# The last step of a layer norm on ScalarE, and its mean folded into the square

## The chip, the cores and the metric

One core of a Trainium2 chip runs the whole program. The metric is the device time of one execution in microseconds (us), lower is better. The engines are named as the profile names them: PE (TensorE matmul), PEld (TensorE weight load), DVE (VectorE), ACT (ScalarE), POOL (GpSimd) and SP (SyncE, which issues all DMAs here).

## What is computed

Three layers follow one another: an attention with a small state, a feed-forward layer with softmax-linear units and a layer norm (`_moe_ref`), and a feed-forward layer with squared relu (`_moe2_ref`). The change touches the middle one:

```python
def _moe_ref(x, w_in, w_out, g_ln):              # x: 4352 tokens of 512
    h = x @ w_in                                 # 1024 wide
    e = np.exp(h - h_max)
    solu = h * (e / (np.sum(e) + 1e-09))
    mu = np.mean(solu)
    var = np.mean((solu - mu) ** 2)
    ln = (solu - mu) / np.sqrt(var + 1e-06) * g_ln
    return ln @ w_out
```

All data is fp32; the big products split each operand into a rounded high part and a rest, and take three passes over them.

## The kernel before

**Tiling.** The tokens are taken in 8 batches of 512, four chunks of 128 tokens each, and two more chunks for the states at the end: 34 chunks in all. A chunk has its 128 tokens on the partitions and the 1024 hidden values of each along the free axis, in one tile `u`.

**Stages.** The first stage (the first 430 us of the profiled execution) computes attention and the middle layer. Its loop runs over the batches `b`; each iteration has eight steps `k`, one for each 128 of the 1024 hidden values. In a step, PE transposes the four chunks' finished `u` (`emit_lnT`, L684, into `lnTp`), ACT and DVE write the transposed tile as high part and rest into `lt` (L690 on ACT, then L693 on DVE), and PE multiplies the `lt` of the step before with `w_out` (`emit_l2`, L719, 12 matmuls into `y`). Between these come the first product of the next batch (`emit_l1`, L632, one chunk in each of four steps), the attention of the batch after that (`sT`, `ep`, `aT`, `srd`, `xs`, `sw`), and the decoding of the third layer's weights (`raw`, `dec`, `w2s`, with L312, L315, L318, and `copy` L262 and `sub` L268). The transposes of batch b+1 begin in step 7 of iteration b and need all four finished `u`. The second stage (430 us to the end) is the third layer, and uses nothing that the change touches.

**One chunk.** After its two halves are copied out of PSUM with a running minimum (`least`, L387, DVE), `solu_rest` does the rest: exp with the sum `es` on ACT (L592); the product of `u` and `e` with its sum `us` on DVE (L597); the negative mean `nmu` from `us`, a 128x1 operation on DVE (L600); the square of `u + nmu` with its sum `vs` on ACT (L603); four 128x1 operations on POOL (L611 to L618) that leave the reciprocal root in `c` (the tile `vs`); and last `u = (u + nmu) * c` (L621), on DVE or POOL, whichever is free earlier.

**What sets the order.** Each engine runs its instructions in the order in which the program emits them. PE's order is written out in the loops. For the others a planner (`Flow`) holds the open tasks; each request gives engines with a cost (`{"V": 0.75, "P": 1.7}`), and the planner emits it when its model says that operand and engine are free, the most urgent first. So a changed cost or engine of one request moves others too, and those DMAs on SP that depend on them.

Of the kernel before, what the change touches and what calls it, by code (L numbers as in the profile page):

```python
# [11 lines left out]
AF = mybir.ActivationFunctionType  # L12
ALU = mybir.AluOpType
# [151 lines left out]
def attn_solu_relu2_kernel(  # L165
# [14 lines left out]
    nc = tc.nc  # L180
# [6 lines left out]
    B, P, T, _ = x_n.shape  # L187
# [5 lines left out]
    DM, F1 = w_in.shape  # L193
# [388 lines left out]
    def solu_rest(u, nmx, last):  # L582
        def small(name):
            return smp.tile([P, 1], F32, tag=name, name=name, bufs=4)

        yield None, 0.0, lambda: last["done"] is not None
        f = last["done"]
        yield take("e")
        e_ = ep.tile([P, F1], F32, tag="e", name="e")
        es, us, nmu, vs = (small(n) for n in ("es", "us", "nmu", "vs"))  # L590
        q, c = es, vs
        f = yield {"A": 1.16}, f, lambda e: nc.scalar.activation(  # L592
            out=e_, in_=u, func=AF.Exp, bias=nmx, scale=-1.0, accum_out=es
        )

        def prod(e):
            nc.vector.scalar_tensor_tensor(  # L597
                out=u, in0=u, scalar=-1.0, in1=e_, op0=ALU.mult, op1=ALU.mult, accum_out=us
            )
            nc.vector.tensor_scalar(out=nmu, in0=us, scalar1=-1.0 / F1, scalar2=None, op0=ALU.mult)  # L600

        f = yield {"V": 1.33}, f, prod
        f = yield {"A": 1.16}, f, lambda e: nc.scalar.activation(  # L603
            out=e_, in_=u, func=AF.Square, bias=nmu, accum_out=vs
        )
        give("e")

        def root(e):  # L610
            nc.gpsimd.tensor_scalar(  # L611
                out=q, in0=es, scalar1=1e-9, scalar2=1e-3, op0=ALU.add, op1=ALU.mult
            )
            nc.gpsimd.tensor_tensor(out=q, in0=q, in1=q, op=ALU.mult)
            nc.gpsimd.tensor_scalar(
                out=c, in0=vs, scalar1=1.0 / F1, scalar2=q, op0=ALU.mult, op1=ALU.add
            )
            nc.gpsimd.tensor_tensor(out=c, in0=c, in1=mhalf, op=ALU.pow)  # L618

        f = yield {"P": 2.4}, f, root  # L620
        f = yield {"V": 0.75, "P": 1.7}, f, lambda e: eng_of[e].tensor_scalar(  # L621
            out=u, in0=u, scalar1=nmu, scalar2=c, op0=ALU.add, op1=ALU.mult
        )
        return f

# [752 lines left out]
```

## Time and profile before

| | before |
|---|---|
| median of three timed runs | 1113.36 us (1108.63 to 1115.36) |
| profiled execution | 1106.97 us, span 1105.2 us |
| mean granted clock of TensorE | 0.988 |
| busy: PE / DVE / ACT / POOL | 1067.7 / 803.5 / 557.0 / 163.3 us |
| busy of 385 us from 45 to 430: PE / DVE / ACT / POOL | 367.5 / 303.8 / 242.7 / 149.2 us |
| busy of 655.2 us from 450 to the end: PE / DVE / ACT / POOL | 650.4 / 450.1 / 276.9 / 0 us |

A busy time adds up the spans of an engine's instructions without overlap. PEclk is the clock that TensorE was granted, as a part of full speed (2.4 GHz); 0.50 is the lower of its two levels (1.2 GHz). A waiting instruction holds up all that stands behind it on its engine.

### The profile page before, as it was taken

To read this page: it belongs to the slowest core of one execution; us is meant where nothing else is said; L and a number is where in the kernel's file an instruction comes from. 1 tells how busy PE (TensorE), PEld (TensorE's weight loads), DVE (VectorE), ACT (ScalarE), POOL (GpSimd) and SP (SyncE) were. 2 spreads that over 40 slices of the span, in tenths; PEclk is the share of its full clock that TensorE was granted. 3 is DMA by queue.
4 is the path that set the end of the run, shared out by engine and by line. 5 is a ranking of instruction groups with operands and counts; after the bars stand their busy time and mean duration, and the time that the engine had idled before them with its cause. 6 is when DMAs were issued, how large, how long until landed. Compare 5 with 4: busy or idle time off the path is not lost.

```text
span 1105.2 us, 19405 instructions
## 1 busy us (share of the span) xinstructions
PE 1067.7 (97%) x7184; PEld 940.0 (85%) x7184; DVE 803.5 (73%) x1293; ACT 557.0 (50%) x960; POOL 163.3 (15%) x211
## 2 busy tenths in 40 slices
PE   4889999999999899999999999999999999999998
PEld 1467777767777688889998889999999999999998
DVE  6967789787797767877974578755688467855773
ACT  4846576676676546445453334543345334533442
POOL 1623245354453520000000000000000000000000
PEclk8989999999999899999999999999999999999999
DMA  9421464735625457998687767778888888898884
GB/s 350 166 84 44 155 240 148 276 123 208 236 91 218 173 180 241 303 329 278 188 254 226 194 195 213 229 221 273 252 274 289 291 254 274 273 305 253 252 257 153
DMA packets 126509, 247.70 MB, mean 224 GB/s; under 512 B 13520, under 2 KB 36048, under 8 KB 124368
## 3 DMA queue, kind: packets, MB, share of 16 engines
q1 hardware_dynamic: 126416, 246.47, 68.6%
q8 instruction: 57, 0.93, 0.4%
q14 instruction: 36, 0.29, 0.1%
HBM read 199.23 MB, written 47.19 MB: 223 GB/s over the span
## 4 chain that ended last, share of the span: by engine, by line
PE 78%; DVE 8%; DMA 6%; issue 3%; ACT 2%; POOL 2%; SPq 0%; ACTq 0%; POOLq 0%; DVEq 0%
PE h L1286 31%; PE h L1141 30%; PE y L719 10%; PE hps L632 4%; DMA w_d<-w2s 2%; DMA raw<-w_in 2%; DVE u L597 2%; PE lnTp L684 1%; DMA raw<-w_out 1%; DVE u L387 1%; PE hps L376 1%; DMA raw_u<-w_in 1%; POOL w2s L268 1%; DVE dec L318 1%; DVE lt L693 1%
## 5 line engine op out<-in xcount | busy, mean ns | idle before, releaser
L1286 PE MATMUL h<-w,g 128*128 128x256 f32 x2856 | 343.5, 283 | 0.0
L1286 PEld LDWEIGHTS h<-w,g 128*128 128x128 f32 x2856 | 343.3, 192 | 0.2
L1141 PE MATMUL h<-yt,w 128*128 128x384 f32 (+1 forms) x1680 | 328.2, 356 | 0.5 <-ACT ys L262 0.5
L1141 PEld LDWEIGHTS h<-yt,w 128*128 128x128 f32 x1680 | 300.5, 188 | 27.0 <-ACT ys L262 0.7
L719 PE MATMUL y<-lt,wo 128*128 128x512 f32 (+1 forms) x864 | 220.9, 397 | 3.6 <-DVE lt L693 3.3
L262 ACT CAST g<-r 128x768 fp32r<-128x768 f32 (+1 forms) x140 | 128.3, 920 | 149.5 <-PE h L1286 148.0
L719 PEld LDWEIGHTS y<-lt,wo 128*128 128x128 f32 x864 | 150.8, 192 | 40.8 <-issue 6.7
L268 DVE TENSOR_TENSOR g<-r,g 128x768 fp32r<-128x768 f32 (+1 forms) x140 | 148.4, 1063 | 51.0 <-ACT g L262 50.4
L1105 DVE TENSOR_TENSOR r<-u,h 128x384 f32<-128x384 f32 (+1 forms) x120 | 72.1, 604 | 110.2 <-PE h L1141 109.8
L1091 ACT COPY u<-h 128x512 f32<-128x512 f32 (+2 forms) x160 | 81.8, 524 | 112.8 <-PE h L1141 86.6
L1187 DVE TENSOR_TENSOR r<-r 128x768 f32<-128x768 f32 (+1 forms) x100 | 104.9, 1060 | 20.5 <-ACT r L1177 20.2
L632 PE MATMUL hps<-sw,aT 128*128 128x512 f32 x368 | 98.1, 415 | 0.6 <-DVE s_sb L387 0.6
L632 PEld LDWEIGHTS hps<-sw,aT 128*128 128x128 f32 x368 | 69.0, 190 | 24.4 <-issue 5.8
L693 DVE SCALAR_TENSOR_TENSOR lt<-lnTp,g_sb,lt 128x512 fp32r<-128x512 f32 (+1 forms) x72 | 51.4, 714 | 27.0 <-ACT lt L690 26.7
L690 ACT ACTIVATE lt<-lnTp,g_sb 128x512 fp32r<-128x512 f32 (+1 forms) x72 | 47.7, 663 | 42.3 <-PE lnTp L684 42.2
L1179 DVE SCALAR_TENSOR_TENSOR r<-r 128x768 f32<-128x768 f32 (+3 forms) x80 | 65.2, 835 | 1.2
L1091 ACT ACTIVATE r<-h 128x384 f32<-128x384 f32 (+1 forms) x40 | 21.3, 532 | 83.1 <-PE h L1141 82.7
L603 ACT ACTIVATE e<-u,nmu 128x1024 f32<-128x1024 f32 x34 | 39.1, 1149 | 20.9 <-DVE nmu L600 20.9
L684 PE MATMUL lnTp<-ident,u 128*128 128x128 f32 x272 | 42.8, 277 | 4.9 <-DVE u L621 2.8
L597 DVE SCALAR_TENSOR_TENSOR u<-u,e 128x1024 f32<-128x1024 f32 x34 | 44.0, 1295 | 4.0 <-ACT e L592 4.0
L268 DVE TENSOR_TENSOR yt<-yraw,yt 128x384 fp32r<-128x384 f32 (+1 forms) x70 | 41.3, 606 | 6.3 <-ACT yt L262 6.2
L268 POOL TENSOR_TENSOR w2s<-dec,w2s 128x512 fp32r<-128x512 f32 (+1 forms) x30 | 35.9, 1197 | 60.9 <-ACT w2s L262 59.7
(97 smaller groups left out, 922.4 us busy)
## 6 DMA issues: line engine op xcount, KB each, us to landing
w<-w_d SPq DMA_DIRECT2D x560, 256.0 KB, 3.3
w_d<-w2s SPq DMA_DIRECT2D x36, 512.0 KB, 3.8
raw<-w_out SPq DMA_DIRECT2D x24, 512.0 KB, 6.8
xT<-x_t SPq DMA_DIRECT2D x8, 1024.0 KB, 6.9
xn<-x_n SPq DMA_DIRECT2D x8, 1024.0 KB, 5.9
y_d<-ys SPq DMA_DIRECT2D x16, 512.0 KB, 3.2
raw<-w_in SPq DMA_DIRECT2D x16, 512.0 KB, 6.8
out<-u SPq DMA_DIRECT2D x28, 256.0 KB, 2.8
```

Source lines behind the costliest of these rows:

```text
L262: nc.scalar.copy(out=out, in_=in_)
L268: return lambda e: eng_of[e].tensor_tensor(out=out, in0=in0, in1=in1, op=ALU.subtract)
L597: nc.vector.scalar_tensor_tensor(out=u, in0=u, scalar=-1.0, in1=e_, op0=ALU.mult, op1=ALU.mult, accum_out=us)
L632: nc.tensor.matmul(out=ps, lhsT=lhsT(i, k), rhs=rhs(j, k)[:, cs], start=(k == 0 and n == 0), stop=(k == n_k - 1 and n == len(passes) - 1),)
L693: f = yield {"V": 0.1 + nt * 0.155}, f, lambda e: nc.vector.scalar_tensor_tensor(out=o[:, 1], in0=pf, scalar=gk, in1=o[:, 0].bitcast(F32), ...
L719: nc.tensor.matmul(out=ps, lhsT=wo[k][:, w, c * P:(c + 1) * P], rhs=o[:, a], start=(k == 0 and i == 0), stop=(k == K1 - 1 and i == 2),)
L1091: nc.scalar.activation(out=o, in_=src, func=func) if func else nc.scalar.copy(out=o, in_=src)
L1105: f = yield {"V": 0.15 + cols / 960}, max(at, box["task"]["done"]), lambda e: nc.vector.tensor_tensor(out=o, in0=box["t"], in1=src, op=ALU.add
L1141: nc.tensor.matmul(out=ps, lhsT=wt[:, e2, k], rhs=yy[:, e1, k], start=(p in ("P1", "P2", "P5") and k == 0 and s == 0), stop=(k == 1 and s ...
L1179: f = yield {"V": 0.15 + (2 - key[-1]) * q / 960}, f, lambda e: nc.vector.scalar_tensor_tensor(out=v, in0=v, scalar=0.0, in1=v, op0=ALU.ma ...
L1187: return lambda e: eng_of[e].tensor_tensor(out=out, in0=in0, in1=in1, op=op)
L1286: nc.tensor.matmul(out=where[i // 2][0][:, i % 2 * Q:i % 2 * Q + Q], lhsT=g[:, e1, m % 2, i * P:i * P + P], rhs=wt[:, e2], start=(p in ("P ...
```

## The change

The mean is no operation of its own any more. The square takes the sum `us` as its bias and `-n` as its scale (n = 1024), so that it sums (us - n u)^2, and the factor n^-3 in the third small POOL operation takes that back to the variance. POOL gets a fifth small operation, `nmu = -us / n * c`, and the last step becomes one ACT activation, `u = c * u + nmu`. The planner's costs change with it: 1.3 for the product, 2.7 for the root, and 1.16 on ACT alone for the last step.

```diff
         def prod(e):
             nc.vector.scalar_tensor_tensor(
                 out=u, in0=u, scalar=-1.0, in1=e_, op0=ALU.mult, op1=ALU.mult, accum_out=us
             )
-            nc.vector.tensor_scalar(out=nmu, in0=us, scalar1=-1.0 / F1, scalar2=None, op0=ALU.mult)
-
-        f = yield {"V": 1.33}, f, prod
+
+        f = yield {"V": 1.3}, f, prod
         f = yield {"A": 1.16}, f, lambda e: nc.scalar.activation(
-            out=e_, in_=u, func=AF.Square, bias=nmu, accum_out=vs
+            out=e_, in_=u, func=AF.Square, bias=us, scale=-n, accum_out=vs
         )
...
             nc.gpsimd.tensor_scalar(
-                out=c, in0=vs, scalar1=1.0 / F1, scalar2=q, op0=ALU.mult, op1=ALU.add
+                out=c, in0=vs, scalar1=n ** -3, scalar2=q, op0=ALU.mult, op1=ALU.add
             )
             nc.gpsimd.tensor_tensor(out=c, in0=c, in1=mhalf, op=ALU.pow)
-
-        f = yield {"P": 2.4}, f, root
-        f = yield {"V": 0.75, "P": 1.7}, f, lambda e: eng_of[e].tensor_scalar(
-            out=u, in0=u, scalar1=nmu, scalar2=c, op0=ALU.add, op1=ALU.mult
+            nc.gpsimd.tensor_scalar(
+                out=nmu, in0=us, scalar1=-1.0 / n, scalar2=c, op0=ALU.mult, op1=ALU.mult
+            )
+
+        f = yield {"P": 2.7}, f, root
+        f = yield {"A": 1.16}, f, lambda e: nc.scalar.activation(
+            out=u, in_=u, func=AF.Identity, bias=nmu, scale=c
         )
```

Counted over the whole program, DVE loses the 34 means, 10 of the last steps and 8 subtractions `w2s`, and gets two copies from ACT; POOL loses 24 of the last steps and gets 34 small operations and the 8 subtractions; ACT gets 34 activations and gives up the two copies. PE's order is the same, instruction for instruction. In the new kernel the lines from L592 on carry other numbers: exp L593, product L598, Square L603, the last step L624, `lt` L693 on ACT and L696 on DVE.

At the start, ACT's rows from the second chunk's square to the transposed tile of batch 0. Before, where the last step is on no ACT row:

```order
L603 ACTIVATE e,vs<-u,nmu 128x1024
L262 CAST wo_136<-dec 128x512
L592 ACTIVATE e,es<-u,hm 128x1024
L504 ACTIVATE sr<-srd,l_190 128x64 x2
L400 ACTIVATE eT,l_472<-s_sb,m_491 128x512
L262 COPY xs<-xsp 128x4x32
L262 CAST sw<-hps 128x512
L400 ACTIVATE eT,l_472<-s_sb,m_492 128x512
L262 COPY s_sb<-ep 128x512
L603 ACTIVATE e,vs<-u,nmu 128x1024
L262 COPY s_sb<-ep 128x512
L433 ACTIVATE a_sb<-a_sb 128x512
```

And now, at the same place:

```order
L593 ACTIVATE e,es<-u,hm 128x1024
L504 ACTIVATE sr<-srd,l_190 128x64 x2
L603 ACTIVATE e,vs<-u,us 128x1024
L400 ACTIVATE eT,l_477<-s_sb,m_490 128x512
L262 COPY xs<-xsp 128x4x32
L603 ACTIVATE e,vs<-u,us 128x1024
L262 COPY s_sb<-ep 128x512
L624 ACTIVATE u<-u,nmu,vs 128x1024
L400 ACTIVATE eT,l_477<-s_sb,m_491 128x512
L624 ACTIVATE u<-u,nmu,vs 128x1024 x2
L262 CAST sw<-hps 128x512
L693 ACTIVATE lt<-lnTp,g_sb 128x512
```

The last chunk's square stands two attention rows (`L400`, `s_sb`) earlier, three last steps stand behind it, and the softmax rows of the next batch's attention (`L433 a_sb`) come behind the first `lt` instead of ahead of it.

In iteration 3, ACT's rows around two successive `lt`. Before:

```order
L312 ACTIVATE dec<-raw 128x512
L433 ACTIVATE a_sb<-a_sb 128x512
L312 ACTIVATE dec<-raw 128x512
L603 ACTIVATE e,vs<-u,nmu 128x1024
L690 ACTIVATE lt<-lnTp,g_sb 128x512
L592 ACTIVATE e,es<-u,hm 128x1024
L262 COPY s_sb<-ep 128x512
L400 ACTIVATE eT,l_2232<-s_sb,m_2246 128x512
L433 ACTIVATE a_sb<-a_sb 128x512
L603 ACTIVATE e,vs<-u,nmu 128x1024
L690 ACTIVATE lt<-lnTp,g_sb 128x512
```

And now:

```order
L312 ACTIVATE dec<-raw 128x512
L433 ACTIVATE a_sb<-a_sb 128x512
L603 ACTIVATE e,vs<-u,us 128x1024
L693 ACTIVATE lt<-lnTp,g_sb 128x512
L312 ACTIVATE dec<-raw 128x512
L593 ACTIVATE e,es<-u,hm 128x1024
L262 COPY s_sb<-ep 128x512
L400 ACTIVATE eT,l_2224<-s_sb,m_2239 128x512
L624 ACTIVATE u<-u,nmu,vs 128x1024
L433 ACTIVATE a_sb<-a_sb 128x512
L603 ACTIVATE e,vs<-u,us 128x1024
L693 ACTIVATE lt<-lnTp,g_sb 128x512
```

The second decode (`L312`, which waits for a `raw` DMA) moves behind the first `lt`, and between the two `lt` there are now seven activations instead of five.

At the end of iteration 6, DVE's rows from the last chunk's second half (`hps,hm`) to the `lt` of step 7. `wil` are subtractions that only the last two chunks need later. Before:

```order
L387 TENSOR_SCALAR u,hm<-hps,hm 128x512
L693 SCALAR_TENSOR_TENSOR lt<-lnTp,g_sb,lt 128x512
L268 TENSOR_TENSOR wil<-wi_126,wih 128x512
L268 TENSOR_TENSOR wil<-wi_127,wih 128x512
L597 SCALAR_TENSOR_TENSOR u,us<-u,e 128x1024
L600 TENSOR_SCALAR nmu<-us 128x1
L693 SCALAR_TENSOR_TENSOR lt<-lnTp,g_sb,lt 128x512
```

And now:

```order
L387 TENSOR_SCALAR u,hm<-hps,hm 128x512
L696 SCALAR_TENSOR_TENSOR lt<-lnTp,g_sb,lt 128x512
L268 TENSOR_TENSOR wil<-wi_128,wih 128x512
L268 TENSOR_TENSOR wil<-wi_129,wih 128x512
L598 SCALAR_TENSOR_TENSOR u,us<-u,e 128x1024
L696 SCALAR_TENSOR_TENSOR lt<-lnTp,g_sb,lt 128x512
L268 TENSOR_TENSOR wil<-wi_126,wih 128x512
L696 SCALAR_TENSOR_TENSOR lt<-lnTp,g_sb,lt 128x512
```

The last chunk's half and product stand one `lt` and two `wil` earlier than they did, and one `wil` takes the product's place ahead of step 7's `lt`.

## Rows read from the trace of the kernel before

**Rows 1.** Busy time by stretch: length, PE, PEld, DVE, ACT, POOL, clock, DMA share, GB/s.

```profile
45.00:430.00 385.00, 367.52 (x2526) 284.60 (x2514) 303.84 (x612) 242.69 (x454) 149.20 (x192) 0.98 0.48 171
450.00:1105.20 655.20, 650.37 (x4451) 627.13 (x4449) 450.07 (x592) 276.94 (x442) 0.00 (x0) 1.00 0.81 251
```

**Rows 2.** Waits of PE, whole span: us in total, times, the longest.

```profile
PE sTp L414 <- DVE lt L693: 5.1, 3, 2.3
PE y L719 <- DVE lt L693: 3.3, 4, 1.9
PE lnTp L684 <- DVE u L621: 2.8, 1, 2.8
...
PE lnTp L684 <- POOL u L621: 1.7, 1, 1.7
```

**Rows 3.** Groups by line: busy us, mean ns of one, idle before.

```profile
L603 ACT ACTIVATE e<-u,nmu 128x1024 f32<-128x1024 f32 x34 | 39.1, 1149 | 20.9 <-DVE nmu L600 20.9
L621 POOL TENSOR_SCALAR u<-u,nmu,vs 128x1024 f32<-128x1024 f32 x24 | 34.7, 1444 | 2.5
L621 DVE TENSOR_SCALAR u<-u,nmu,vs 128x1024 f32<-128x1024 f32 x10 | 8.4, 841 | 1.5 <-POOL vs L618 1.5
L600 DVE TENSOR_SCALAR nmu<-us 128x1 f32<-128x1 f32 x34 | 5.2, 154 | 1.2
L615 POOL TENSOR_SCALAR vs<-vs,es 128x1 f32<-128x1 f32 x34 | 11.7, 345 | 68.7 <-ACT e L603 68.4
L268 POOL TENSOR_TENSOR w2s<-dec,w2s 128x512 fp32r<-128x512 f32 (+1 forms) x30 | 35.9, 1197 | 60.9 <-ACT w2s L262 59.7 <-DMA w_d<-w2s 1.2
```

**Rows 4.** The start, in order of time, PE and DVE: start, us, [idle before].

```profile
58.16 0.95 PE L684 MATMUL lnTp<-ident,u 128*128 128x128 f32 x5 [2.78 <-DVE u L621]
61.22 2.07 PE L719 MATMUL y<-lt,wo 128*128 128x512 f32 x4 [0.73 <-DVE lt L693]
...
57.39 0.72 DVE L621 TENSOR_SCALAR u<-u,nmu,vs 128x1024 f32<-128x1024 f32 x1
```

**Rows 5.** Iteration 3, in order of time: ACT and PE.

```profile
218.09 0.68 ACT L312 ACTIVATE dec<-raw 128x512 f32<-128x512 f32 x1 [1.41 <-DMA raw<-w_in]
220.22 0.68 ACT L312 ACTIVATE dec<-raw 128x512 f32<-128x512 f32 x1 [0.93 <-DMA raw<-w_in]
221.92 0.68 ACT L690 ACTIVATE lt<-lnTp,g_sb 128x512 fp32r<-128x512 f32 x1
228.12 0.67 ACT L690 ACTIVATE lt<-lnTp,g_sb 128x512 fp32r<-128x512 f32 x1
...
223.44 0.66 PE L414 MATMUL sTp<-ident,s_sb 128*128 128x128 f32 x4 [2.34 <-DVE lt L693]
```

**Rows 6.** Busy time between the two `lt` of ACT in iteration 3, columns as above.

```profile
221.92:228.12 6.20, 4.68 (x25) 3.99 (x26) 5.26 (x11) 4.78 (x12) 2.93 (x5) 1.00 0.00 0
```

**Rows 7.** The turn from iteration 6 to 7, in order of time: PE, DVE, POOL.

```profile
366.95 3.44 PE L719 MATMUL y<-lt,wo 128*128 128x512 f32 x14
372.29 1.79 PE L719 MATMUL y<-lt,wo 128*128 128x512 f32 x4 [1.90 <-DVE lt L693]
376.41 0.47 PE L684 MATMUL lnTp<-ident,u 128*128 128x128 f32 x1 [1.69 <-POOL u L621]
376.54 2.91 PE L719 MATMUL y<-lt,wo 128*128 128x512 f32 x6
...
366.99 2.16 DVE L268 TENSOR_TENSOR wil<-wi,wih 128x512 fp32r<-128x512 f32 x2
369.07 2.31 DVE L597 SCALAR_TENSOR_TENSOR u<-u,e 128x1024 f32<-128x1024 f32 x1
...
374.63 1.72 POOL L621 TENSOR_SCALAR u<-u,nmu,vs 128x1024 f32<-128x1024 f32 x1
```

**Rows 8.** Busy time and granted clock in two stretches, columns as above.

```profile
60.00:65.00 5.00, 4.27 (x13) 3.10 (x12) 3.18 (x7) 0.59 (x1) 1.30 (x2) 0.50 0.00 0
375.00:380.00 5.00, 3.59 (x12) 2.89 (x13) 4.31 (x6) 3.04 (x6) 4.36 (x3) 0.55 0.57 224
```

More of the change, by code (lines that the diff above doesn't have):

```diff
@@ L591, in solu_rest @@
         q, c = es, vs
+        n = float(F1)
         f = yield {"A": 1.16}, f, lambda e: nc.scalar.activation(
```

## The prediction

> **What bounds the kernel now.** I read the table of stretches first. PE is busy for 650.4 of the 655.2 us after 450, and PE's order is the same in both kernels, so nothing is to be gained or lost there [rows 1]. From 45 to 430 PE is busy for 367.5 of 385.0 us: 17.5 us of idle time are what better placed work could give back, and every new wait of PE in that stretch is a loss. DVE works 303.8 us there (79%), ACT 242.7 (63%), POOL 149.2 (39%). So PE is the bound all along, and the other engines count only where PE waits for them.
>
> The list of PE's waits says where that is [rows 2]: 5.1 us in three waits of `sTp` for DVE's `lt`, 3.3 in four waits of `y` for it, and 2.8 and 1.7 in two waits for a finished `u`. These make 12.9 of the 17.5 us. The rest waits for attention tiles.
>
> **What is removed, added and moved.** First the chain of one chunk, with no queue in it. The mean on DVE goes, 0.154 us ahead of the square. POOL's fifth small operation comes in; the trace does not hold it, and its nearest row is L615, the same form with a scalar operand from a tile, at 0.345 us; the bounds are 0.154 (the mean as DVE ran it) and twice the row, 0.69. The last step becomes an activation; the nearest row is the square, with the same shape and one operand from a tile fewer, at 1.149 us, in place of 1.444 on POOL (24 times) and 0.841 on DVE (10 times) [rows 3]. With these the chain changes by -0.154 + 0.345 + 1.149 - 1.444 = -0.10 us for 24 chunks, and by -0.154 + 0.345 + 1.149 - 0.841 = +0.50 for 10. In the mean that is +0.07 us per chunk: as a chain the change gives nothing. What it can give comes from the queues.
>
> The queues: DVE loses 34 x 0.154 + 10 x 0.841 = 13.6 us, and the 8 subtractions that go to POOL besides. POOL loses 34.7, and gets 34 x 0.345 + 8 x 1.197 = 21.3. ACT gets 34 x 1.149 = 39.1 us, and goes from 63% of the stretch to (242.7 + 39.1) / 385 = 73%, DVE from 79% to 75% or less. No engine passes PE over the whole stretch; the local steps decide.
>
> The Trainium skill prices this activation a little higher (ScalarE: Activation LUTs, What ACT_TABLE_LOAD costs): 186 ns + 0.833 ns an element, and 93 ns for each operand from a tile, an estimate of 1.23 us for 1024 elements and two operands. The square's row with one such operand agrees with it (1.13 by the page, 1.149 by the row), and 34 x 0.08 would put 2.7 us more on ACT, or 0.3 in an iteration.
>
> *The start.* PE's transposes for batch 0 wait 2.78 us until 58.16 for the last chunk's `u`, which DVE finishes at 57.39 + 0.72 = 58.11; then `y` waits until 61.22 for the rest part of `lt`, which lies behind other work on DVE [rows 4]. In the new order the last chunk's square stands ahead of two attention rows, and three last steps follow on ACT. Going down ACT's rows with the durations above, I get the last `u` at about 56.5, 1.6 earlier, and `lt`'s rest right behind it on DVE, some 2.8 earlier. The softmax rows (`L433`) now come behind the first `lt`, so the attention transposes that PE needs next are late instead; I take 2.0 of the 2.8. Bounds: 0 (the softmax takes it all) and 2.78 + 0.73 = 3.5 (both waits go).
>
> *The loop.* The largest of the three `sTp` waits is 2.34 us at 223.44 [rows 5]. DVE's `lt` is late because ACT's is (221.92), and that stands behind a square and, ahead of it, two decodes that wait for DMAs (1.41 and 0.93 us). The new order puts one last step ahead of the first decode, where it fits into the 1.41 us for which ACT waits for the DMA anyway, and the second decode, with 0.93 + 0.68 us, behind the `lt`. So this `lt` comes about 1.5 us earlier. Such a saving can't exceed its own wait, and the other two waits are some 1.4 each; I take 1.5 + 1.0 + 1.0 = 3.5 of 5.1 us (bounds 0 and 5.1). Where the cover fails, that is where the DMA has landed before ACT comes to the decode, the step costs its 1.149 us in full and the saving is 0.5.
>
> *The turn from iteration 6 to 7.* `y` waits 1.90 us for `lt` at 372.29, and a transpose 1.69 for the last `u` at 376.41 [rows 7]. Both stand behind one product on DVE, at 369.07 for 2.31 us. In the new order that product stands an `lt` and two subtractions (2.16 us in the trace) earlier, and `lt` is behind one subtraction and no longer behind the product. From the product to the finished `u` it takes 1.15 + 0.19 for the square and its sum, some 1.3 for POOL and 1.15 for the last step, 3.8 us. With the product ending at 368.4 or a little earlier, `u` is there at about 372.1, when PE comes to the transposes. Of 3.6 us I take 3.2 (bounds 0 and 3.6).
>
> *The clock.* In two short stretches TensorE is granted the lower level of its clock: 0.50 of full speed from 60 to 65 and 0.55 from 375 to 380 [rows 8], in both behind PE's idle time. Six matmuls took 2.91 us there and four 1.79, where 14 at full speed took 3.44: 6 x (0.485 - 0.246) + 4 x (0.448 - 0.246) = 2.2 us. If the turn's idle time goes, most of this goes too; I take 2.0 (bounds 0 and 2.2). At the start idle time stays, so I take nothing (bounds 0 and about 4, twice that sum, by the 5 us at 0.50).
>
> *New waits.* ACT is fuller, and each `lt` on it can be late behind a last step. Between the two `lt` at 221.92 and 228.12 ACT was busy for 4.78 of 6.20 us [rows 6]; the new order has one last step and one decode more there, 4.78 + 1.15 + 0.68 = 6.6, or about 6.3 where they overlap their neighbours by 0.1 each. This is the tightest place, and it comes once per iteration. PE has 12 matmuls of 0.246, 2.95 us [rows 7], between the transposes and the use of an `lt`, and `lt` takes 0.68 on ACT and as much on DVE: some 1.5 us of delay are hidden, and a slip of 0.1 to 0.4 is paid for in few steps. I put 2.0 us over all (bounds 0 and 0.4 x 7 = 2.8 without the rival below). The 8 subtractions that move to POOL delay SP's stores of `w2s` and the `raw` loads behind them on its queue; POOL is idle for 60% of the stretch, and a decode now stands later on ACT, so I price that at nothing; without that cover a `raw` load comes 1.197 us later.
>
> **Sum.** 2.0 + 3.5 + 3.2 + 2.0 - 2.0 = 8.7 us. The profiled execution took 1107.0 us, and would take 1098.3; the timed runs have a median of 1113.4, 6.4 above it. I take the saving from the median: 1113.4 - 8.7 = 1104.7 us.
>
> **Rivals.**
> - *Nothing comes of it* (0.25). The chain of one chunk is not shorter, and the `lt` waits are set by `raw` DMAs that no order of ACT speeds up. For it: the +0.07 us, and the waits in [rows 5]. Against: the turn's waits come from DVE's queue [rows 7], where no DMA is. Time: 1113, within 4.
> - *All waits go, and both clock stretches* (0.20). 3.5 + 5.1 + 3.6 + 2.2 + 4 = 18.4 us: 1095, between 1092 and 1100. For it: all of them stand behind `u` or `lt`. Against: some idle time at the start stays in my walk, and the clock fell there.
> - *ACT becomes the bound of the loop, and the kernel is slower* (0.10). The place is the pair of steps with a first product, a decode and attention rows on ACT. If the stall for `raw` (1.41 + 0.93) is not covered any more and adds to the 6.6 us of work in 6.2, ACT ends 2.7 us late, 1.2 beyond what PE can hide, and again in the step behind it: 2.4 x 7 = 17 us, 1130. It decides from about 1.5 us of delay on. For it: ACT's share of the tightest step. Against: the step ahead of it got a decode less. The Trainium skill would expect this one (ScalarE: Activation LUTs, Rules for kernel authors): it says that adds and multiplications belong on VectorE and not on ScalarE. The rows agree as to the single instruction, 0.841 against 1.149, but only 10 of 34 ran on DVE.
>
> **How the numbers follow.** The forecast, 5 to 13 us saved, has 0.45. The range from 1093 to 1116 leaves out the fastest third of the second rival (0.07), the third one (0.10) and a little of the first: about 0.2. One per cent is 11 us, about what a measurement of this kernel can tell from no change. Faster by more, under 1102.2, takes the second rival and a third of the forecast: 0.36. Slower by more takes most of the third rival: 0.09. The rest, 0.55, is within 1%.
>
> **What would show it.** In the new profile the last step should take 1.15 to 1.25 us on ACT, and POOL's fifth operation 0.2 to 0.7. PE's waits for `sTp` should fall from 5.1 us to under 2, those at the turn from 3.6 to under 1, with no clock under 0.9 near 375. The span of the second stage should stay at 655 within 1. I am wrong if PE's idle time from 45 to 430 is still 17 us, or if it waits for ACT's `lt` in most iterations.

## The result and the profile after

The changed kernel takes 1096.07 us (median of 6 runs, 1094.58 to 1096.98) against 1113.59 us for the kernel before in the same set (6 runs, 1108.63 to 1115.36): a ratio of 0.9855, with a 95% interval from 0.9831 to 0.9879. The profiled execution took 1096.98 us, with a span of 1095.1; that of before took 1106.97, with a span of 1105.2. So the two medians are 17.5 us apart, and the two profiled executions 10.0. Both numbers matter below. One execution of the kernel before, in the set of e10, took 1435.67 us at a mean clock of 0.687 and is left out of every comparison.

The line numbers after the change are up to three higher: the last step is L624, POOL's fifth operation L619, and `lt` is made on L693 and L696. The first view after is the table of stretches: length, busy time of each engine, granted clock, DMA share and GB/s. It answers to [rows 1] and [rows 8].

```profile
core 0: us, PE busy (x) PEld busy (x) DVE busy (x) ACT busy (x) POOL busy (x), PEclk, DMA share, GB/s
45.00:430.00 385.00, 375.53 (x2563) 293.13 (x2552) 294.43 (x573) 279.91 (x494) 129.21 (x208) 0.99 0.50 177
370.00:380.00 10.00, 10.00 (x50) 8.28 (x49) 7.61 (x13) 4.38 (x9) 5.12 (x5) 1.00 0.68 267
60.00:65.00 5.00, 5.00 (x17) 4.02 (x17) 2.67 (x5) 1.36 (x3) 3.52 (x3) 0.50 0.02 3
178.00:181.00 3.00, 3.00 (x10) 2.42 (x9) 2.56 (x4) 2.71 (x5) 0.40 (x2) 0.50 0.00 0
```

PE now sits idle for 9.5 of the 385 us, where it was 17.5. ACT has gone from 242.7 to 279.9 us and is at 73%; PE is not waiting for it more than before. The low clock near 375 is gone. The one behind 60 is still there, and there is a new one from 178 to 181 us, where the kernel before is granted 1.00.

The second view is the list of PE's waits over the whole span (in total, times, the longest), which answers to [rows 2].

```profile
...
PE sTp L414 <- DVE lt L696: 3.3, 1, 3.3
PE y L722 <- DVE sw L268: 1.7, 2, 1.1
...
PE lnTp L687 <- ACT u L624: 1.1, 2, 0.8
PE xsp L519 <- ACT sr L504: 1.0, 1, 1.0
...
PE y L722 <- DVE lt L696: 0.3, 1, 0.3
...
```

The 12.9 us of waits for `lt` and `u` have become 3.3 + 1.1 + 0.3 = 4.7, with 1.7 us of a new wait for `sw`, a part of the attention, at the start. What is left in the loop is one single wait of 3.3 us.

The third view is the groups by line, for the operations whose price the prediction had to take from neighbours [rows 3].

```profile
L624 ACT ACTIVATE u<-u,nmu,vs 128x1024 f32<-128x1024 f32 x34 | 42.1, 1241 | 2.5 <-POOL nmu L619 2.5
L603 ACT ACTIVATE e<-u,us 128x1024 f32<-128x1024 f32 x34 | 39.0, 1148 | 5.7 <-DVE u L598 5.5
L619 POOL TENSOR_SCALAR nmu<-us,vs 128x1 f32<-128x1 f32 x34 | 15.1, 445 | 3.5
```

The last step takes 1.241 us and the fifth small operation 0.445, where I had taken 1.149 and 0.345. The square waits 5.7 us in all for what comes ahead of it, where it waited 20.9: the mean no longer stands between the product and the square.

The fourth view is PE's longer waits in order of time, from 45 us to the end of the first stage: start, duration, tile and, in brackets, the wait.

```profile
47.92 0.33 PE L519 MATMUL xsp<-ident,sr 128*128 128x128 f32 x1 [1.00 <-ACT sr L504]
...
55.62 0.76 PE L687 MATMUL lnTp<-ident,u 128*128 128x128 f32 x5 [0.80 <-ACT u L624]
...
59.15 1.65 PE L722 MATMUL y<-lt,wo 128*128 128x512 f32 x3 [1.13 <-DVE sw L268]
177.59 0.93 PE L414 MATMUL sTp<-ident,s_sb 128*128 128x128 f32 x4 [3.29 <-DVE lt L696]
...
421.06 11.17 PE L1144 MATMUL h<-yt,w 128*128 128x512 f32 x48 [0.54 <-ACT ys L262]
```

Between 178 and 407 us PE doesn't wait at all. The turn from iteration 6 to 7, with its 1.90 and 1.69 us [rows 7], passes without a gap. The second stage begins at 421.06 instead of 430.19 us, and from there to the end it takes 674.0 us instead of 675.0. The difference of 1.0 us lies behind PE's last matmul, which ends 4.8 us ahead of the end of the span before and 3.9 now; up to there the second stage is as it was.

### The profile page after: what moved, and what is told of

Read it like the earlier page. It is cut to its first block, busy times and chain, and to the rows that moved or that the text cites. A ratio compares the mean times of both kernels' runs of the same rounds, so it can differ in the third digit from the quotient of the medians.

```text
span 1095.1 us, 19407 instructions
## 1 busy us (share of the span) xinstructions
PE 1065.5 (97%) x7184; PEld 941.0 (86%) x7184; DVE 786.7 (72%) x1243; ACT 589.4 (54%) x992; POOL 144.2 (13%) x229
## 4 chain that ended last, share of the span: by engine, by line
PE 89%; ACT 4%; DVE 3%; DMA 2%; issue 1%; POOL 1%; SPq 0%; ACTq 0%; DVEq 0%; POOLq 0%
PE h L1289 31%; PE h L1144 30%; PE y L722 15%; PE hps L635 7%; PE lnTp L687 2%; PE hps L376 1%; DMA raw_u<-w_in 1%; ACT u L624 1%; PE aTp L470 1%; DMA raw<-w_in 1%; ACT e L603 1%; PE srd L486 1%; PE sTp L414 0%; DMA raw<-w_out 0%; PE sps L376 0%
## 5 line engine op out<-in xcount | busy, mean ns | idle before, releaser
L696 DVE SCALAR_TENSOR_TENSOR lt<-lnTp,g_sb,lt 128x512 fp32r<-128x512 f32 (+1 forms) x72 | 51.6, 716 | 25.6 <-ACT lt L693 24.8
L1182 DVE SCALAR_TENSOR_TENSOR r<-r 128x768 f32<-128x768 f32 (+3 forms) x80 | 65.2, 834 | 1.2
L693 ACT ACTIVATE lt<-lnTp,g_sb 128x512 fp32r<-128x512 f32 (+1 forms) x72 | 47.7, 662 | 31.4 <-PE lnTp L687 31.3
L268 POOL TENSOR_TENSOR w2s<-dec,w2s 128x512 fp32r<-128x512 f32 (+1 forms) x38 | 47.9, 1273 | 70.3 <-ACT w2s L262 50.3
L598 DVE SCALAR_TENSOR_TENSOR u<-u,e 128x1024 f32<-128x1024 f32 x34 | 42.5, 1249 | 5.9 <-ACT e L593 5.5
L624 ACT ACTIVATE u<-u,nmu,vs 128x1024 f32<-128x1024 f32 x34 | 42.1, 1241 | 2.5 <-POOL nmu L619 2.5
```

The lines of the kernel that those rows point to most:

```text
L268: return lambda e: eng_of[e].tensor_tensor(out=out, in0=in0, in1=in1, op=ALU.subtract)
L624: f = yield {"A": 1.16}, f, lambda e: nc.scalar.activation(out=u, in_=u, func=AF.Identity, bias=nmu, scale=c)
L1182: f = yield {"V": 0.15 + (2 - key[-1]) * q / 960}, f, lambda e: nc.vector.scalar_tensor_tensor(out=v, in0=v, scalar=0.0, in1=v, op0=ALU.ma ...
```

## The experiments

My theory after the result was that of the prediction, sharpened. The loop waits where ACT, which runs its work strictly in order, has a decode (L312) ahead of an `lt`, and the decode's `raw` DMA has not landed. The change moves decodes behind the `lt`, and the turn is freed of one late product. The rivals: it is the load taken from VectorE or from POOL, or it is the fold of the mean.

### The kernel before against itself

The unchanged kernel, to see what a difference of this size is worth and how far its executions differ.

> The kernel before, unchanged, so that its executions are seen with their clock. Theory 1 (its executions differ: idle time of PE before a transpose or an attention tile sometimes brings a further stretch at the lower clock): times of 1107 to 1116 us, and the longer ones at a lower mean clock, 0.988 for 1107 and 0.980 or less for 1114. Theory 2 (the profiled execution of this kernel was just a lucky one in its DMA waits): the same spread at an unchanged clock of 0.988. Theory 3 (a profiled execution is always some 6 us faster than a timed one): the profile is again at 1107 and every timed run at 1113.

Measured: 1110.77 us (12 runs, 1107.49 to 1115.54), ratio 1.0 (0.9983 to 1.0017). The executions of before differ by 8 us among themselves, and the three longest (1112.81, 1114.16 and 1115.54) have the lowest mean clock, 0.984, against 0.985 to 0.989 for the others: the first theory holds in part. The third is refuted, since the profiled execution is above the median here. It took 1112.53 us, 5.6 more than the profiled one that the prediction was read from, and its list of PE's waits has this row:

```profile
PE sTp L414 <- DVE lt L693: 7.5, 4, 2.4
```

That is four waits and 7.5 us, against three and 5.1 in [rows 2]. In iterations 3 to 6 (180 to 360 us) ACT stood 16.8 us ahead of its 16 decodes in this execution, and 13.6 in the other. So 2.4 of the 5.6 us are the very waits that the change is about: the execution I predicted from was one with few of them. Of the rest, 1.5 us are a low stretch of the clock behind one of these waits (0.51 from 223.2 to 226.6 us), and 1.2 lie in the second stage, which the change does not touch.

### The two halves of the change apart

e1 moves the last step to ScalarE and leaves the mean where it was; against the kernel before:

```diff
-
-        f = yield {"P": 2.4}, f, root
-        f = yield {"V": 0.75, "P": 1.7}, f, lambda e: eng_of[e].tensor_scalar(
-            out=u, in0=u, scalar1=nmu, scalar2=c, op0=ALU.add, op1=ALU.mult
+            nc.gpsimd.tensor_scalar(
+                out=nmu, in0=nmu, scalar1=c, scalar2=None, op0=ALU.mult
+            )
+
+        f = yield {"P": 2.7}, f, root
+        f = yield {"A": 1.16}, f, lambda e: nc.scalar.activation(
+            out=u, in_=u, func=AF.Identity, bias=nmu, scale=c
```

> One part alone: the last step runs on ACT, the mean stays an operation of DVE ahead of the square, and POOL multiplies it by the root. Theory 1 (queues: taking 34.7 us off POOL and 8.4 off DVE lets the tiles of the turn and the start come earlier): most of the gain, 1097 to 1101 us, and no wait of PE at the turn from iteration 6 to 7. Rival (it is the 0.154 us mean between product and square that held ACT up, 20.9 us of idle time of ACT before the square): at most a third of the gain, 1107 or more.

Measured: 1093.09 us (1091.92 to 1093.93), ratio 0.9835 (0.981 to 0.9859). That is all of the gain, and some 3 us more than the changed kernel has.

e2 is the other half, the mean folded into the square and the last step where it was; against the changed kernel:

```diff
             nc.gpsimd.tensor_scalar(
-                out=nmu, in0=us, scalar1=-1.0 / n, scalar2=c, op0=ALU.mult, op1=ALU.mult
+                out=nmu, in0=us, scalar1=-1.0 / n, scalar2=None, op0=ALU.mult
             )
...
-        f = yield {"A": 1.16}, f, lambda e: nc.scalar.activation(
-            out=u, in_=u, func=AF.Identity, bias=nmu, scale=c
+        f = yield {"V": 0.75, "P": 1.7}, f, lambda e: eng_of[e].tensor_scalar(
+            out=u, in0=u, scalar1=nmu, scalar2=c, op0=ALU.add, op1=ALU.mult
```

> The other part alone: the sum goes into the square, the mean is a fifth operation on POOL, and the last step stays on DVE or POOL. Theory 1 (queues): POOL's chain gets 0.4 us longer and the last steps stay in the two queues that made PE wait, so little is gained: 1108 to 1116 us. Rival (the mean between product and square): 1097 to 1103 us.

Measured: 1108.87 us (1106.05 to 1112.06), ratio 0.9981 (0.9965 to 0.9997): 2 us. The waits for `lt` in the loop are all there (8.4 us in four). The 5.2 us that VectorE saves on the mean are hidden nearly whole.

### How much room ScalarE has

e3 adds to the changed kernel a copy of the chunk onto itself on ScalarE, behind the last step, 34 times:

```diff
             out=u, in_=u, func=AF.Identity, bias=nmu, scale=c
         )
+        f = yield {"A": 1.1}, f, lambda e: nc.scalar.copy(out=u, in_=u)
```

> The changed kernel with one more pass of ACT over each finished tile, a copy in place of 1.1 us, planned for at that cost: it measures how much room ACT has. By the prediction's third rival ACT is close to its limit in the steps with a first product, and another 34 x 1.1 = 37 us on it make PE wait for lt in most iterations: 1110 us or more. If ACT still has room (its share goes from 74% to 84% of the stretch) the copies are hidden but for the start and the turn: 1097 to 1103 us.

Measured: 1123.92 us (1122.32 to 1124.69), ratio 1.0108 (1.0079 to 1.0138). The loss is not where my rival of a slower kernel had put it. PE's list of waits, and ACT in order of time near 410 us:

```profile
PE y L723 <- ACT lt L694: 21.3, 2, 16.4
PE lnTp L688 <- ACT u L627: 7.5, 7, 2.6
```

```profile
410.50 0.62 ACT L262 CAST w2s<-dec 128x512 fp32r<-128x512 f32 x1 [1.45 <-DVE dec L318]
414.50 0.62 ACT L262 CAST w2s<-dec 128x512 fp32r<-128x512 f32 x1 [2.58 <-DVE dec L268]
415.03 0.68 ACT L694 ACTIVATE lt<-lnTp,g_sb 128x512 fp32r<-128x512 f32 x1
```

From 180 to 360 us PE was busy for all 180.00 us: there the loop takes one more ScalarE step per chunk without a wait, with 12 decodes instead of 16. The price is paid at the start, where `u` is late (four of the seven waits, 5.6 of the 7.5 us), and in iteration 7: the weights whose decoding was put off come there all together, and their casts stand ahead of an `lt` and wait for VectorE's half of the decoding. So ACT does not become the bound of iterations 3 to 6, even with twice the addition; but what is put off has to be done somewhere, and in iteration 7 PE does wait for ACT.

### Which load it was: VectorE's or POOL's

e5 allows the last step of the kernel before on POOL alone, e6 on VectorE alone:

```diff
-        f = yield {"V": 0.75, "P": 1.7}, f, lambda e: eng_of[e].tensor_scalar(
+        f = yield {"P": 1.7}, f, lambda e: eng_of[e].tensor_scalar(       # e5
+        f = yield {"V": 0.75}, f, lambda e: eng_of[e].tensor_scalar(      # e6
```

> The kernel before, with the last step allowed on POOL alone: 10 of the 34 go from VectorE to POOL, ScalarE is as before. This takes VectorE's part of the last step away (10 x 0.841 = 8.4 us) without ScalarE. Theory 1 (the gain of the change is what VectorE's queue lost: lt came late behind the last steps there): a good part of the gain comes here too, 1098 to 1105 us, with sTp waits under 3 us. Theory 2 (the gain is that the last step is done sooner than POOL's 1.44 us behind POOL's other work lets it): POOL gets 14.4 us more, no gain, 1110 to 1120, with longer waits of PE for POOL's u.

Measured: 1109.99 us (1107.38 to 1114.66), ratio 0.9996 (0.9978 to 1.0013). From PE's list of waits:

```profile
PE lnTp L684 <- POOL u L621: 4.5, 1, 4.5
PE sTp L414 <- DVE lt L693: 4.4, 3, 2.5
```

The waits of the loop are nearly those of before, and the `u` that POOL now finishes more often alone costs 4.5 us at one place.

> The kernel before, with the last step allowed on VectorE alone: 24 of the 34 go from POOL (1.444 us each) to VectorE (0.841), ScalarE is as before, and the planner gives 14 subtractions of w2s to POOL in turn. The counterpart of e5. Theory 1 (what counts is that the finished u comes soon, without POOL's 1.4 us and POOL's other work ahead of it): the waits for u go, a good part of the gain comes here too, 1097 to 1104 us. Theory 2 (what counts is VectorE's queue, in which lt stands): VectorE gets 24 x 0.841 = 20 us more and loses some 10, lt comes later, 1112 to 1122, with more and longer waits for lt. Theory 3 (both: one queue is relieved and the other filled, only ScalarE has room for it): 1108 to 1113, the waits for u gone and those for lt grown by as much.

Measured: 1106.26 us (1103.46 to 1110.74), ratio 0.9965 (0.9946 to 0.9984). From the same list:

```profile
PE sTp L414 <- DVE lt L693: 7.4, 3, 3.0
PE lnTp L684 <- DVE u L621: 5.3, 2, 2.7
```

POOL is relieved, and the waits for `lt` and `u` are longer than before. Neither engine's relief brings the gain: e5 takes the last step from VectorE, e6 takes it from POOL, and 0 and 4 us come of it.

### The bound: no last step at all

e12 leaves the last step of the kernel before out:

```diff
         f = yield {"P": 2.4}, f, root
-        f = yield {"V": 0.75, "P": 1.7}, f, lambda e: eng_of[e].tensor_scalar(
-            out=u, in0=u, scalar1=nmu, scalar2=c, op0=ALU.add, op1=ALU.mult
-        )
         return f
```

> The kernel before with the last step left out altogether (its output lacks the layer norm's scaling and shift). It takes 34.7 us from POOL and 8.4 from VectorE and puts nothing anywhere: the bound of what any place for the last step can give. Theory 1 (on ScalarE the last step is hidden whole): as e7 and e1 within 2 us, 1090 to 1095. Theory 2 (ScalarE's 34 x 1.24 us are paid for in part, at the start and in the waits for lt): under 1088.

Measured: 1102.9 us (1098.37 to 1105.66), ratio 0.9926 (0.9894 to 0.9958). Neither theory had this: the kernel without the last step is some 7 us slower than the changed kernel, and some 10 slower than e1, which differs from it in the last step on ScalarE and the small POOL operation that goes with it. Work taken away is therefore not where most of the gain comes from. PE's waits in e12, and ACT's decodes from 180 to 360 us:

```profile
PE sTp L414 <- DVE lt L690: 5.6, 4, 2.1
PE y L716 <- DVE lt L690: 3.9, 4, 2.8
```

```profile
L312 ACT ACTIVATE dec<-raw 128x512 f32<-128x512 f32 x16 | 10.6, 661 | 11.9 <-DMA raw<-w_out 6.5 <-DMA raw<-w_in 5.4
```

The waits for `lt` are all there, 5.6 us against the 5.1 of [rows 2], and ACT still stands 11.9 us ahead of 16 decodes. The longest of the waits of `y`, 2.8 us, is at the turn from iteration 6 to 7.

### The same operations in another order

The changed kernel and e1 differ by 3 us; e7 tells the fold and the order apart. It is the changed kernel with one number of the planner put back, and its order then is that of e1, operation for operation, on every engine:

```diff
-        f = yield {"V": 1.3}, f, prod
+        f = yield {"V": 1.33}, f, prod
```

> The changed kernel again, beside e11 and e7 on one chip, since the difference of 3 us between the changed kernel (1096.07) and e1 (1093.09) comes from two different sets of runs. If that difference is real: 1095 to 1098 us here, with one wait of sTp for DVE's lt of about 3 us near 178 in the profile, and 2 to 4 us above e11. If it was only the set of runs: within 1 us of e11.

> e1 again (the last step alone on ScalarE; the mean stays a VectorE operation and the square is as before), beside e10 and e7. Expected 1092 to 1094 us, no wait of sTp for lt over 0.5 us in the loop, one wait of y for lt of about 2 us near 379.

> The changed kernel with one number of the planner put back (the product's cost 1.33 instead of 1.30). The order on every engine then is that of e1, operation for operation, and what is left between the two is the fold alone: 34 small operations of VectorE are gone, the square has a scale, and POOL's last small operation reads the sum. Theory 1 (the order makes the 3 us): as e11 within 1 us, 1092 to 1094, without the wait of 3.3 us near 178. Theory 2 (the fold itself costs it, because VectorE's and POOL's small operations change their place in time): as e10, 1095 to 1098, in spite of the order. Theory 3 (the fold is worth its 34 x 0.154 = 5.2 us of VectorE): under 1091.

Measured on one chip: the changed kernel 1095.39 us (4 runs, 1092.24 to 1096.54), e1 1092.47 (1091.70 to 1094.08), e7 1092.52 (1091.77 to 1095.35). e7 is as e1: the fold itself is worth nothing here, and the 3 us are the order. With four runs each the ranges overlap, but e1 and the changed kernel were as far apart in their first sets. The place is seen in ACT's rows in order of time, first of the changed kernel, near 170 us:

```profile
170.18 0.66 ACT L312 ACTIVATE dec<-raw 128x512 f32<-128x512 f32 x1
170.74 0.63 ACT L433 ACTIVATE a_sb<-a_sb 128x512 f32<-128x512 f32 x1
174.38 0.66 ACT L312 ACTIVATE dec<-raw 128x512 f32<-128x512 f32 x1 [3.02 <-DMA raw<-w_in]
174.95 1.13 ACT L603 ACTIVATE e<-u,us 128x1024 f32<-128x1024 f32 x1
176.08 0.67 ACT L693 ACTIVATE lt<-lnTp,g_sb 128x512 fp32r<-128x512 f32 x1
```

and the same place in e7:

```profile
168.12 0.66 ACT L312 ACTIVATE dec<-raw 128x512 f32<-128x512 f32 x1
168.69 0.62 ACT L433 ACTIVATE a_sb<-a_sb 128x512 f32<-128x512 f32 x1
169.40 1.15 ACT L603 ACTIVATE e<-u,us 128x1024 f32<-128x1024 f32 x1
170.55 0.67 ACT L693 ACTIVATE lt<-lnTp,g_sb 128x512 fp32r<-128x512 f32 x1
171.94 0.68 ACT L312 ACTIVATE dec<-raw 128x512 f32<-128x512 f32 x1 [0.73 <-DMA raw<-w_in]
```

In the first, ACT waits 3.02 us for a DMA with the square and the `lt` queued behind it, and PE pays 3.29 us at 177.59. In the second the decode stands behind the `lt`, its DMA has landed but for 0.73 us by the time ACT comes to it, and PE waits for nothing there. In the repeat e10 the first wait is there again, with 2.35 us. The wait is not the whole price: a low stretch of the clock stands behind it, in e10 and e8 too. Laid against e7 matmul by matmul, the changed kernel loses 5.1 us at this place. It gets 2.2 back later, since e7, like e1 and e11, waits 2.0 us for an `lt` near 378, where the changed kernel does not wait.

### Two attempts at a better order

e8 gives the planner the last step's price as measured, e13 takes e7 and puts the attention's last multiplication of the first batch on VectorE:

```diff
-        f = yield {"A": 1.16}, f, lambda e: nc.scalar.activation(
+        f = yield {"A": 1.25}, f, lambda e: nc.scalar.activation(         # e8, last step
-            f = yield {"P": 1.2, "V": 0.69}, f, lambda e: eng_of[e].tensor_tensor(
+            f = yield {"P": 1.2, "V": 0.69} if b else {"V": 0.69}, f, lambda e: eng_of[e].tensor_tensor(   # e13
```

> The changed kernel with one number of the planner changed: the last step's cost is 1.25, as the trace has it (1.241), in place of 1.16. No operation changes, only the order and a copy or two between engines. Theory 1 (the wait of 3 us near 178 is the planner's order, set by a cost that is too low): the wait goes, 1091 to 1094. Theory 2 (the order that comes out is a matter of luck, a better cost doesn't make it better): 1094 to 1098, with a wait somewhere of 2 us or more.

Measured: 1097.39 us (1095.70 to 1097.54), ratio 0.988 (0.9851 to 0.9909), with the wait near 177 us as before (2.87 us). A truer price does not give a better order.

> e7 with the attention's last multiplication of the first batch (a times 1/sum) on VectorE instead of POOL, an attempt at a version that beats both kernels. PE waits 7.3 us for it in two waits at the start, in every kernel so far; POOL takes 1.05 and 1.30 us, and VectorE's price for the same is not in the trace of that place (0.68 for the subtraction of the same shape). Expected 0.4 to 0.6 us less in each of the two waits, 1091.5 at the best; since the planner's order changes with it, 1090 to 1095.

Measured: 1098.64 us (1097.18 to 1103.87), ratio 0.9903 (0.9865 to 0.9941). It gains 0.8 us at the wait it was meant for (6.5 instead of 7.3 us) and loses 6. It has the last step on ScalarE, and yet the loop's waits of the kernel before are back. ACT in iteration 3, PE, and ACT's decodes from 180 to 360 us:

```profile
216.50 0.67 ACT L312 ACTIVATE dec<-raw 128x512 f32<-128x512 f32 x1 [1.52 <-DMA raw<-w_in]
217.07 0.61 ACT L433 ACTIVATE a_sb<-a_sb 128x512 f32<-128x512 f32 x1
218.11 0.67 ACT L312 ACTIVATE dec<-raw 128x512 f32<-128x512 f32 x1 [0.43 <-DMA raw<-w_in]
218.68 1.14 ACT L603 ACTIVATE e<-u,us 128x1024 f32<-128x1024 f32 x1
219.81 0.67 ACT L693 ACTIVATE lt<-lnTp,g_sb 128x512 fp32r<-128x512 f32 x1
...
221.32 0.67 PE L414 MATMUL sTp<-ident,s_sb 128*128 128x128 f32 x4 [2.25 <-DVE lt L696]
```

```profile
L312 ACT ACTIVATE dec<-raw 128x512 f32<-128x512 f32 x16 | 10.6, 664 | 12.3 <-DMA raw<-w_in 6.7 <-DMA raw<-w_out 5.5
```

Two decodes with their waits stand ahead of the square and the `lt`, as in [rows 5], and PE waits 2.25 us at the same place as there (2.34). The turn from iteration 6 to 7 stays short, with one wait of 0.7 us for `u`. The planner's order moved by itself when one operation elsewhere lost a choice.

## What the runs together say

One view sorts the loop's waits: ACT's decodes in iterations 3 to 6 (180 to 360 us, 16 of them in nearly every kernel), with the time ACT stood idle ahead of them, beside PE's waits of `sTp` for `lt` in the same stretch and the spread of the timed runs. The last column needs no waits. PE runs the same 7184 matmuls in the same order in all these kernels, so the time between the same two can be compared: from the one that starts at 172.02 us in before to the one at 363.02 (the end of iteration 2 and iterations 3 to 6), and from there to the one at 431.23 (the turn and iteration 7).

| kernel | idle ahead of decodes, us | PE's `sTp` waits, us | timed runs, us | PE from 172 to 363, from 363 to 431, us |
|---|---|---|---|---|
| before, first profile / e0 | 13.6 / 16.8 | 3.8 / 6.4 | 1107.5 to 1115.5 (e0) | 191.0, 68.2 / 195.1, 68.1 |
| e2, fold alone | 15.9 | 4.9 | 1106.1 to 1112.1 | 197.2, 65.2 |
| e5, last step on POOL | 11.1 | 1.9 | 1107.4 to 1114.7 | 194.6, 69.2 |
| e6, last step on VectorE | 12.6 | 7.4 | 1103.5 to 1110.7 | 197.3, 67.0 |
| e12, no last step | 11.9 | 3.5 | 1098.4 to 1105.7 | 193.3, 66.4 |
| e13, on ScalarE, another order | 12.3 | 4.0 | 1097.2 to 1103.9 | 191.9, 62.2 |
| e8, changed, price 1.25 | 7.1 | 0.0 | 1095.7 to 1097.5 | 190.6, 61.4 |
| changed kernel / e10 | 5.5 / 5.5 | 0.0 / 0.0 | 1094.6 to 1097.0 / 1092.2 to 1096.5 | 189.7, 61.5 / 189.0, 61.4 |
| e7, e1, e11 | 4.9, 4.2, 5.0 | 0.0 each | 1091.7 to 1095.4 | 184.6 to 185.1, 63.1 each |
| e3, a copy more (12 decodes) | 3.4 | 0.0 | 1122.3 to 1124.7 | 184.3, 90.4 |

In this stretch every kernel with 11 us or more of such idle time has waits of PE, every one with 7.1 or less has none, and this cuts across the engines: e13 has the last step on ScalarE and belongs to the upper half, with its four runs 6.7 us apart. The stretch leaves out iteration 2, where the changed kernel, e10 and e8 have one wait each, of 3.29, 2.35 and 2.87 us. Over the whole loop (62 to 420 us, 24 decodes) the upper half has 18.5 to 25.6 us of idle time and 4.4 to 8.4 us of waits, the lower half 11.3 to 16.8 and 0 to 3.3: the same order of kernels, with a smaller gap. The upper kernels spread by 6 to 8 us over their timed runs, the lower ones by 2 to 4 (there are more runs of some of the former, but e12 with six and e13 with four spread as far). A DMA lands a little earlier or later from one execution to the next, and where a decode stands ahead of an `lt`, PE pays for it. That reading of the spread is argued from the table; only the two profiles of before show it in rows.

The last column tells two gains apart. From 363 us on, the kernels divide by the engine of the last step and not by their decodes: 61.4 to 63.1 us with it on ScalarE, e13 among them, and 65.2 to 69.2 without, even where it is left out (e12). Only e3 falls out, with its put-off decodes. Between the two profiled executions that the prediction is about, this part brings 6.7 us and the stretch from 172 to 363 only 1.3. In that stretch it is e1, e7 and e11 that gain, some 6 us against the first profile of before and 10 against e0.

Three things stay open. Why the turn is short in the four orders that have the last step on ScalarE, and in none of the other five, is not taken apart; relief of POOL and VectorE alone is not the reason, since e12 has both and waits 2.8 us there. A kernel with the last step where it was and only the decodes moved behind the `lt` was not tried, so it is not shown that the order alone would bring the loop's part in the old kernel. And why the planner puts decodes behind when ScalarE has the last step in its plan is only argued: a fuller ScalarE in the plan makes decodes, which nobody waits for soon, the ones to be put off.

## Why the prediction was right, and where it was not

The time of 1096.07 us lies in the range, but near its fast end. The saving is twice the forecast, 17.5 us instead of 8.7, and with 1.45% it is in the class of faster by over 1%, to which I gave 0.36 against 0.55 for within 1%.

**The baseline** is the step that failed most. The sum itself was close: 8.7 us against 10.0 between the two profiled executions. I then subtracted it from the median of before, as if each execution could save the same. Before's profiled execution lay 6.6 us under its set's median, and after's 0.9 over its own: 10.0 + 6.6 + 0.9 = 17.5. The execution I read was one with short waits, as e0 shows (5.1 us of `sTp` waits here, 7.5 there), and those are what the change takes away. That a slow execution of before had more to give is argued from these two profiles. A part of the 17.5 us is luck of the set as well: over 12 to 23 runs in each of the later sets before has medians of 1110.1 to 1110.9, not 1113.59, and in the set of e10 the medians are 1110.05 and 1095.39, 14.7 us apart.

**The start** was put at 2.0 us. PE's idle time from 45 to 62 us went from 7.1 to 5.2, so the sum of the waits is right; its parts are not all mine. PE's wait for the last `u` fell by 1.7 us (2.8 to 1.1); the tile itself came 2.5 earlier (55.6 instead of 58.1), where I had 1.6. `y` lost its waits for `lt` (0.7 and 0.2) and gained 1.7 for `sw`, whose rows on ACT now stand behind the last steps and among the softmax rows that I had feared. That `xsp` would wait 1.3 us less I had not seen. The low clock behind 60 us stayed, as assumed, but not at the old price: PE now has 5.00 us of work from 60 to 65 and not 4.27, and its lead over before shrank there by 1.1 us. My bounds for the clock there, 0 to 4 us gained, left no room for a loss.

**The loop** was put at 3.5 of 5.1 us; 1.8 came, since the waits fell to 3.3, and the sign that I had named, under 2, failed. The reading of iteration 3 was right to the row: the first wait of ACT for a DMA vanished behind a last step, the second decode went behind the `lt`, and its wait now hurts nobody:

```profile
219.79 1.15 ACT L603 ACTIVATE e<-u,us 128x1024 f32<-128x1024 f32 x1 [0.17 <-DVE u L598]
221.09 0.69 ACT L693 ACTIVATE lt<-lnTp,g_sb 128x512 fp32r<-128x512 f32 x1
223.47 0.68 ACT L312 ACTIVATE dec<-raw 128x512 f32<-128x512 f32 x1 [1.69 <-DMA raw<-w_in]
```

The wait of 2.34 us went whole. What I got wrong is that the other waits would shrink alike. The order is laid out for each iteration anew; in iteration 2 it set a decode ahead of the `lt`, and 1.37 us at 176.74 became 3.29 at 177.59. e7 shows what there was to get, 0.2 us of such waits over the whole span; its twin in order, e11, has 1.6 in its profile. Both have the 2.0 us for an `lt` near 378 instead.

**The turn** was put at 3.2 of 3.6 us. All of it went, and the 0.45 us at 364.20 too: 4.0 us. The reason was right: the product on VectorE that took 2.31 us at 369.07 [rows 7] runs earlier, and for less:

```profile
361.34 1.23 DVE L598 SCALAR_TENSOR_TENSOR u<-u,e 128x1024 f32<-128x1024 f32 x1
362.49 0.75 DVE L696 SCALAR_TENSOR_TENSOR lt<-lnTp,g_sb,lt 128x512 fp32r<-128x512 f32 x1
```

**The clock** at the turn came back as forecast, 1.00 from 370 to 380 us where it was 0.55 in a part of it; of the 2.2 us that the stretch had cost I had taken 2.0. But a low stretch came elsewhere, behind the wait of 3.29 us. The same matmuls of PE before, at 1.00, and now, at 0.50:

```profile
177.16 0.94 PE L719 MATMUL y<-lt,wo 128*128 128x512 f32 x3
177.93 2.92 PE L632 MATMUL hps<-sw,aT 128*128 128x512 f32 x12
...
178.17 1.63 PE L722 MATMUL y<-lt,wo 128*128 128x512 f32 x3
179.59 3.71 PE L635 MATMUL hps<-sw,aT 128*128 128x512 f32 x12
```

That is 1.5 us more, for which the sum has no term.

**New waits** were put at 2.0 us over the steps with two `lt`. No wait of that kind is to be seen. The two `lt` of the tightest step now begin at 221.09 and 229.15, and ACT is busy for 6.37 us between them: I had the work right (6.3 to 6.6) and the room wrong, since the first of them came 0.8 us earlier than before and the second 1.0 later, and PE still did not wait for it. What came in place of these waits is the longer one in iteration 2 with its clock, 1.9 + 1.5 = 3.4 us, and it has another cause: a decode and its DMA.

**The sum, place by place.** Since PE's order is the same, the lead of the changed kernel can be read at any matmul:

| the same matmul of PE | before, us | changed, us | lead, us |
|---|---|---|---|
| start, `srd` | 45.92 | 45.24 | 0.7 |
| start, `y`, ahead of most of the low stretch | 62.66 | 60.17 | 2.5 |
| `y`, behind the low stretch | 68.05 | 66.62 | 1.4 |
| iteration 2, `sTp`, behind its wait | 176.74 | 177.59 | -0.8 |
| iteration 2, `lnTp`, behind the new low stretch | 180.69 | 183.14 | -2.5 |
| iteration 3, `sTp` | 223.44 | 223.41 | 0.0 |
| ahead of the turn, `y` | 363.02 | 360.60 | 2.4 |
| behind the turn, `y` | 381.16 | 371.94 | 9.2 |
| first matmul of the second stage | 430.19 | 421.06 | 9.1 |
| end of the span | 1105.19 | 1095.13 | 10.1 |

Until the wait in iteration 2 the lead was 1.1 us, where I had 2.0 for the start. From there to 363 us it grew by 1.3; I had 3.5 - 2.0 = 1.5 for the loop and the new waits. The turn and its clock brought 6.8, where I had 5.2. The 1.0 us at the end I did not have. So the forecast of 8.7 us against 10.1 rests on the turn, where the mechanism was right. That the loop fits to 0.2 is luck. I had 1.7 us too much for the `lt` waits and nothing for the 1.5 of the clock; on the other side stand the 2.0 of waits that did not come and 0.6 at an `hps`, gained without my counting on it.

**The prices.** The last step took 1.241 us, not the 1.149 of the square, and the Trainium skill's figures (ScalarE: Activation LUTs, What ACT_TABLE_LOAD costs) agree with it: the estimate from that page was 1.23. In iterations 3 to 6 the 0.09 us more per chunk cost nothing that shows, since e3 hides a whole copy per chunk there; at the start, where PE waits for `u`, no run tells.

**The rivals.** That nothing would come of it is refuted. The second rival named 1095 us, close to what was timed, but by another road: one clock stretch stayed, another came, and 4.7 us of the waits stayed. The slower one, ACT as the bound of the loop, is refuted by e3 for the steps in which I had put it. It drew on the Trainium skill's rule (ScalarE: Activation LUTs, Rules for kernel authors) that adds and multiplications belong on VectorE. The trace agrees as to the single operation, 0.841 us on VectorE and 1.241 on ScalarE; as to the whole kernel the runs go against it here, with 1106.26 us for the last step on VectorE (e6) and 1092.5 for it on ScalarE (e11 and e7).

## What to carry to other kernels

Where engines run in order and a planner lays out the order, a change of one operation's engine is above all a new order: look for what now stands ahead of the work that the bound engine waits for, and first for operations that can wait for a DMA. Leaving the operation out altogether is not the upper bound of such a change; here it was slower than doing it on the engine with room. And before a saving read from one execution is subtracted from a median, compare the two: if the executions differ by just the waits that the change removes, the median has more to save.

## What the runs showed of the hardware

The last step as an activation with both scale and bias from tiles took 1.241 us for 128x1024, the square with its bias alone from a tile 1.148: 0.09 us more with one operand more. The product of 128x1024 on VectorE took 1.23 us at 361.34 us in the changed kernel and 2.31 us at the turn of the kernel before [rows 7]. The table of stretches of before has POOL busy for 2.35 of the 2.50 us there:

```profile
369.00:371.50 2.50, 1.39 (x7) 0.81 (x5) 2.47 (x5) 0.00 (x0) 2.35 (x2) 1.00 0.61 247
```

Over all 34 products the mean went from 1.295 to 1.249 us as POOL lost the large last steps. That the two engines slow each other is what these rows suggest; no run measured it by itself. The clock's low stretch behind 60 us is not a fixed property of the kernel: the profiles of the changed kernel and its repeat show 0.50 and 0.61 from 60 to 65 us, and e11 shows 1.00 with nearly the same waits ahead of it. Nor does a wait of some 2 us always bring one. The waits of 3.29 us in the changed kernel, 2.87 in e8, 2.44 in e0 and 2.35 in e10 have a stretch at 0.50 beside them; 2.34 at 223.44 in before and 1.99 near 378 in e7 have none.
